# A state-space convolution and attention kernel: filter generation and the first FFT convolution put into one pipeline over chunks of 128 channels

## The chip, the cores and the metric

The kernel runs on one core of a Trainium2 chip. The metric is the device time of that core in microseconds (us), as the median of the runs; all runs quoted here are of the same, undisturbed state, and most runs of one kernel lie within 0.5%. The engines are named as the profile names them: PE (TensorE, matrix multiplication; PEld is its weight load), DVE (VectorE), ACT (ScalarE), POOL (GpSimd). SP issues DMA.

## The reference, cut to what matters

Sequence length 2048, 512 channels, 128 complex modes per channel, 32 heads of 16, all in bf16. The output is four residual layers in a row: a state-space convolution A, a sliding-window attention B, the same A again, the same B again.

```python
def _A_ref(u, ...):                       # u is layernorm(x)
    dt = exp(log_dt)
    K = einsum("dn,dnl,dn->dl", C, exp(dt*A*l), dt*B).real    # filter: 512 channels x 2048 taps
    y = irfft(rfft(u padded to 2L) * rfft(K padded to 2L))[:L]
    return y + u * Dskip
def _B_ref(x, wqkv, wo):                  # window of 8 positions, step 2
    ...
x = x + A(ln(x)); x = x + B(ln(x)); x = x + A(ln(x)); x = x + B(ln(x))
```

The filter K is the same in both A layers, so it is made once.

## The kernel before

A tap index l is split as l = x + 32·y, so that a power of the mode is a product of two table entries: table X has the powers 0 to 31, table Y the 64 powers in steps of 32 (with the coefficient folded in). For each channel, K is a small matrix product of Y and X with the 128 modes as the contraction. The tables are made on VectorE by doubling: level `lev` makes entries m..2m−1 from entries 0..m−1 by one complex multiplication, which is four products and two sums.

```python
def dbl_level(T, lev, lad0, dsl):              # 128 channels at a time
    m = 1 << lev
    for e0 in range(0, m, HALF):
        for (r_out, m_a, m_b, op) in ((0, Mr, Mi, ALU.subtract), (1, Mi, Mr, ALU.add)):
            nc.vector.tensor_tensor(ta, T[:, :, 0, e0:e0+mm, :], m_a, ALU.mult)
            nc.vector.tensor_tensor(tb_, T[:, :, 1, e0:e0+mm, :], m_b, ALU.mult)
            nc.vector.tensor_tensor(T[:, :, r_out, m+e0:m+e0+mm, :], ta, tb_, op)

for dc in range(4):                            # kgen: all four chunks of 128 channels
    for lev in range(6): dbl_level(Y, lev, 5, dsl)
    for dch in range(128):                     # contraction, 2 weight loads and matmuls per channel
        nc.tensor.matmul(psk[:, dl, :], Y[:, dh, 0, :, d2], X[:, dh, 0, :, d2], start=True,  stop=False)
        nc.tensor.matmul(psk[:, dl, :], Y[:, dh, 1, :, d2], Xin[:, dh, :, d2],  start=False, stop=True)
    ...                                        # X of the next chunk; k_fft of the chunk before
```

Only when all of K's spectrum is there does the first convolution begin. A transform of 128 channels has a first step (`s1`: 32 matmuls, then copies `Z` out of PSUM) and a second step (`s2`: 16 or 32 PE transposes, a copy `zt`, DFT matmuls with constants `C2`, 512 columns each). The kernel before does the second step in quarters (`cg` counts 16 of them), and lets each quarter's product and inverse follow on the next quarter's forward transform:

```python
for cg in range(17):                            # a_layer, both convolutions
    if cg < 16:
        if c == 0: Z = fft_s1_chunk(...)
        xp = fft_s2_sub(nc, P, C, Z, c)         # 8 transposes, zt, 4 DFT matmuls
        cur = (cg,) + pointwise(cg, xp)         # xc on ACT, pa and pb on DVE
    if pend is not None: inverse_s2(*pend)      # the quarter before
    pend = cur
# then one last stage for all channels, 32 matmuls of 512 plus the skip term T = U*Dskip and X
```

## Time and profile before

The median of the kernel before is 824.7 us in the runs beside the changed kernel (823.9 in the first three). In the stage table below, stage ends are read from the copies that write X in the timeline.

| stage of the profiled execution | from | to | length, us |
|---|---|---|---|
| ladder of powers | 0 | 68 | 68 |
| tables and contraction | 68 | 281 | 213 |
| last filter transform and convolution 1 | 281 | 403.3 | 122 |
| attention 1 | 403.3 | 554.6 | 151.3 |
| convolution 2 | 554.6 | 666.2 | 111.6 |
| attention 2 and store | 666.2 | 826.0 | 159.8 |

The busy line of the page of the kernel before gives averages over all these stages:

```profile
PE 526.4 (64%) x4796; PEld 345.1 (42%) x4848; DVE 583.6 (71%) x989; ACT 314.5 (38%) x368; POOL 6.3 (1%) x5
```

The windows view of the kernel before gives the same by stage. Its columns are named in its first line: each engine's busy us, with the number of instructions in brackets, then the granted PE clock as a share of full speed, the share of DMA engines busy, and GB/s.

```profile
core 0: us, PE busy (x) PEld busy (x) DVE busy (x) ACT busy (x) POOL busy (x), PEclk, DMA share, GB/s
68.00:281.00 213.00, 112.52 (x1357) 93.03 (x1360) 174.14 (x266) 65.22 (x67) 0.00 (x0) 1.00 0.00 1
281.00:403.00 122.00, 94.36 (x745) 66.05 (x753) 85.41 (x187) 57.51 (x81) 6.06 (x1) 0.97 0.17 65
554.60:666.20 111.60, 80.86 (x631) 56.56 (x640) 64.23 (x112) 42.75 (x58) 0.00 (x0) 0.86 0.13 53
```

In the first stage DVE is busy 174 of 213 us: it bounds table building. In the two convolutions no engine is full (PE, the busiest, 77% and 72%). The timeline of the kernel before, PE only, shows two more things (columns: start, duration, engine, line, operation; in brackets the idle time before it and what ended it): a contraction pair, one matmul of the real and one of the imaginary part, and the first matmul of convolution 2.

```profile
105.25 0.21 PE L381 MATMUL psk<-Xtab,Ytab 128*64 128x32 bf16 x1
105.30 0.21 PE L382 MATMUL psk<-Xin,Ytab 128*64 128x32 bf16 x1
...
570.71 1.01 PE L162 MATMUL ps_s_5152<-U_5042,F1sb 128*128 128x128 bf16 x8 [17.40 <-DMA F1sb<-c_F]
```

One weight load with its matmul starts every 53 ns. Convolution 2 starts 16 us after attention 1's last copy, and waits for a DMA of a constant that stands behind the 4 MB filter.

### The profile page before, as it was taken

To read this page: it belongs to the slowest core of one execution; us is meant where nothing else is said; L and a number is where in the kernel's file an instruction comes from. 1 tells how busy PE (TensorE), PEld (TensorE's weight loads), DVE (VectorE), ACT (ScalarE), POOL (GpSimd) and SP (SyncE) were. 2 spreads that over 40 slices of the span, in tenths; PEclk is the share of its full clock that TensorE was granted. 3 is DMA by queue.
4 is the path that set the end of the run, shared out by engine and by line. 5 is a ranking of instruction groups with operands and counts; after the bars stand their busy time and mean duration, and the time that the engine had idled before them with its cause. 6 is when DMAs were issued, how large, how long until landed. Compare 5 with 4: busy or idle time off the path is not lost.

```text
span 826.0 us, 11334 instructions
## 1 busy us (share of the span) xinstructions
PE 526.4 (64%) x4796; PEld 345.1 (42%) x4848; DVE 583.6 (71%) x989; ACT 314.5 (38%) x368; POOL 6.3 (1%) x5
## 2 busy tenths in 40 slices
PE   0200176565655757888699718962888859971996
PEld 0100174462643735665345513432666534551343
DVE  0899979979797367666925989685666373598961
ACT  0431025244152345444564322351444446432234
POOL 0000000000000000002000000000000000000000
PEclk9999999999999999999899859995999969985999
DMA  9000000000000024002000300015000000030011
GB/s 208 8 0 0 0 2 1 1 1 1 2 0 1 2 102 204 1 1 77 27 1 2 90 1 0 1 58 247 2 1 2 1 0 1 2 90 1 0 52 52
DMA packets 8655, 25.61 MB, mean 31 GB/s; under 512 B 4446, under 2 KB 5982, under 8 KB 7518
## 3 DMA queue, kind: packets, MB, share of 16 engines
q1 hardware_dynamic: 4828, 18.16, 6.5%
q10 hardware_dynamic: 3776, 6.72, 2.8%
q8 instruction: 38, 0.62, 0.3%
q14 instruction: 13, 0.11, 0.0%
HBM read 14.95 MB, written 6.29 MB: 26 GB/s over the span
## 4 chain that ended last, share of the span: by engine, by line
PE 44%; DVE 33%; ACT 10%; issue 6%; DMA 6%; ACTq 0%; DVEq 0%; SPq 0%
PE ps_qk L512 7%; DVE ta L313 6%; DVE tb L314 6%; DVE Ytab L315 5%; PE po L623 5%; PE psk L381 3%; PE psk L382 3%; PE ps_v L525 3%; DMA F1sb<-c_F 3%; PE ps_o L640 3%; DVE prodpv L617 2%; ACT xc L220 2%; PE Lp L555 2%; ACT KTq L383 2%; PE vp L234 2%
## 5 line engine op out<-in xcount | busy, mean ns | idle before, releaser
L381 PE MATMUL psk<-Xtab,Ytab 128*64 128x32 bf16 x512 | 56.5, 213 | 83.9 <-issue 60.6
L623 PE MATMUL po<-prodpv,sb_ident 128*128 128x512 bf16 x248 | 66.5, 399 | 35.5 <-DVE prodpv L609 31.3
L381 PEld LDWEIGHTS <-Ytab 128*64 128x64 bf16 x512 | 55.4, 157 | 73.8 <-issue 61.0
L382 PEld LDWEIGHTS <-Ytab 128*64 128x64 bf16 x512 | 55.0, 156 | 27.8 <-DVE Ytab L315 14.0
L382 PE MATMUL psk<-Xin,Ytab 128*64 128x32 bf16 x512 | 56.4, 214 | 13.6 <-DVE Ytab L315 13.6
L512 PE MATMUL ps_qk<-xnT,wqk 128*128 128x512 bf16 x248 | 58.2, 386 | 4.8 <-ACT xnT L499 3.9
L383 ACT CAST KTq<-psk 64x1024 bf16<-64x1024 f32 x16 | 16.1, 1006 | 104.1 <-PE psk L382 104.1
L623 PEld LDWEIGHTS <-sb_ident 128*128 128x128 bf16 x256 | 25.8, 101 | 67.4 <-issue 45.4
L609 DVE TENSOR_TENSOR prodpv<-V,Lsb 128x2048 bf16<-128x2048 bf16 (+1 forms) x40 | 42.2, 1113 | 16.3 <-PE po L623 16.1
L220 ACT CAST xc<-xp 128x1024 bf16<-128x1024 f32 x32 | 32.4, 1012 | 33.6 <-PE xp L188 33.6
L315 DVE TENSOR_TENSOR Ytab<-ta,tb 128x2048 bf16<-128x2048 bf16 (+4 forms) x56 | 42.9, 765 | 1.9
L555 PE MATMUL Lp<-sb_bones,prodqk 128*128 128x8 bf16 x1024 | 34.5, 167 | 12.6 <-DVE prodqk L551 7.2
L178 PE MATMUL pt<-sb_ident,Z 128*128 128x128 bf16 x384 | 39.5, 256 | 4.5 <-ACT Z L361 2.7
L555 PEld LDWEIGHTS <-prodqk 128*128 128x128 bf16 x1024 | 32.3, 98 | 21.7 <-DVE prodqk L551 8.7
L178 PEld LDWEIGHTS <-Z 128*128 128x128 bf16 x384 | 32.4, 117 | 17.9 <-issue 8.0
L512 PEld LDWEIGHTS <-wqk 128*128 128x128 bf16 x256 | 25.3, 100 | 33.9 <-issue 6.9
L234 PE MATMUL vp<-sb_IC,pb 128*128 128x256 bf16 x128 | 36.5, 285 | 3.0 <-DVE pb L224 3.0
L233 PE MATMUL vp<-sb_IC,pa 128*128 128x256 bf16 x128 | 36.4, 284 | 1.8 <-DVE pa L223 1.8
L358 PEld LDWEIGHTS <-F1Ksb 64*128 64x128 bf16 x256 | 27.1, 139 | 24.7 <-issue 20.7
L640 PE MATMUL ps_o<-wo_t,oT 128*128 128x512 bf16 x124 | 32.3, 379 | 6.9 <-ACT o L626 4.3
L235 PE MATMUL vp<-sb_IC,pb 128*128 128x256 bf16 x128 | 36.1, 282 | 0.0
L236 PE MATMUL vp<-sb_IC,pa 128*128 128x256 bf16 x128 | 35.9, 281 | 0.0
(350 smaller groups left out, 1220.2 us busy)
## 6 DMA issues: line engine op xcount, KB each, us to landing
kt_scratch<-Kt_81 SPq DMA_DIRECT2D x1, 4096.0 KB, 12.1
Kt<-kt_scratch SPq DMA_DIRECT2D x1, 4096.0 KB, 14.8
Vp<-V SPq DMA_DIRECT2D x2, 1568.0 KB, 9.0
F1Tsb<-c_F1T ACTq DMA_DIRECT2D x2, 1024.0 KB, 11.4
F1sb<-c_F SPq DMA_DIRECT2D x2, 1024.0 KB, 12.2
F1Ksb<-c_F1K ACTq DMA_DIRECT2D x1, 1024.0 KB, 16.9
wqk<-in_B_wqkv_dram SPq DMA_DIRECT2D x1, 1024.0 KB, 5.7
X_70<-in_A_u_dram SPq DMA_DIRECT2D x1, 512.0 KB, 7.6
```

The source lines that it names most:

```text
L178: nc.tensor.transpose(pt[:, r, g, :], Z[:, r, c * 4 + g, :], ident[:])
L220: nc.scalar.copy(xc[:], xp[:])
L234: nc.tensor.matmul(o, P2, IC[:, 1, :], start=False, stop=False)
L313: nc.vector.tensor_tensor(ta[:, :, 0:mm, :], T[:, :, 0, e0:e0 + mm, :], m_a, ALU.mult)
L314: nc.vector.tensor_tensor(tb_[:, :, 0:mm, :], T[:, :, 1, e0:e0 + mm, :], m_b, ALU.mult)
L315: nc.vector.tensor_tensor(T[:, :, r_out, m + e0:m + e0 + mm, :], ta[:, :, 0:mm, :], tb_[:, :, 0:mm, :], op)
L381: nc.tensor.matmul(psk[:, dl, :], Y[:, dh, 0, :, d2], X[:, dh, 0, :, d2], start=True, stop=False)
L382: nc.tensor.matmul(psk[:, dl, :], Y[:, dh, 1, :, d2], Xin[:, dh, :, d2], start=False, stop=True)
L512: nc.tensor.matmul(ps[:, sc * 512:(sc + 1) * 512], wqk[:, ct, which * 512 + ft * 128: which * 512 + (ft + 1) * 128], xnT[:, ct, s0:s0 + 51 ...
L555: nc.tensor.matmul(Lp[f2][:, w, jj, :], pr[:, f2, jj * 128:(jj + 1) * 128], bones[:], start=True, stop=True)
L623: nc.tensor.matmul(po[jj // 2][:, jj % 2, :], ident[:], p2[:, jj, :], start=(w == 0), stop=(w == W - 1))
L640: nc.tensor.matmul(ps[:, jj, :], oT[:, ft, j * 128:(j + 1) * 128], wo_t[:, ft, :], start=(ft == 0), stop=False)
```

## The change

The intent: hide the first convolution under table building, which leaves PE idle for about half of the time and ACT for more, and make the tables cheaper.

1. Chunks of 128 channels go through one pipeline: tables of the two halves (64 channels each), transform of U, transform of K of the chunk before, and the last part (product, inverse, last matmuls) of the chunk before.
2. The split is now l = y + 64·x. Table Y's last two levels (16 entries to 64) are not doubled but left as unsummed products: the 16 base entries times three multipliers, once by the real part and once by the imaginary part. The sum of the two happens in the contraction, as two more matmuls into the same PSUM cells.
3. The contraction uses 32-column weights in four column groups.
4. The skip term goes into K's spectrum (one matmul with a row of ones), so T and its matmuls go away.
5. K passes through DRAM once to change its layout; the spectrum goes to DRAM for convolution 2, and is loaded after the constants there.

The diff, cut to its core:

```diff
-            for lev in range(6):
-                dbl_level(Y, lev, 5, dsl)
+        for lev in range(4):
+            self.double(Y, 1 << lev, lev, hc)
+        for q, lev in ((1, 4), (2, 5), (3, LV48)):          # y_products
+            nc.vector.tensor_tensor(Y[.. q*EYB:(q+1)*EYB ..], src, self.mult(self.MA, lev, hc, EYB), ALU.mult)
+            nc.vector.tensor_tensor(Y2[.. (q-1)*EYB:q*EYB ..], src, self.mult(self.MB, lev, hc, EYB), ALU.mult)
 ...
+        for ds in range(16):                                # contract, 64 channels
+            for m in range(4):
+                for g in range(4):
+                    d = g * 16 + ds
+                    xs = X[:, m // 2, h, :, t]
+                    if m % 2 == 0:
+                        nc.tensor.matmul(psk[32*g:32*g+32, ds, :], xs, Y[:, m // 2, h, :, t], ...)
+                    else:
+                        nc.tensor.matmul(psk[32*g:32*g+32, ds, EYB:], xs, Y2[:, 1 - m // 2, h, :, t], ...)
 ...
+        for dc in range(4):
+            def mid(dc=dc):
+                xcs[dc] = cv.u_fft(dc, rstd, nb, "act")
+                return k_fft(dc - 1) if dc > 0 else None
+            Kt = half(dc * 2, mid)      # tables of 64 channels, then mid, then the contraction
+            if dc > 0:
+                cv.finish(dc - 1, xcs.pop(dc - 1), Kt)
+            half(dc * 2 + 1)
+        Kt = k_fft(3)
+        cv.finish(3, xcs.pop(3), Kt)
 ...
+    def s2(self, Z, dst, what):                             # second step of every transform
+        for ch in range(2):
+            pt = self.pst([128, 2, 2, 4, 128], BF)
+            ...                                             # 16 transposes into pt
+            self.evac("zt", zt, pt)                         # ACT (DVE in convolution 2)
+            for c2 in range(2):
+                xp = self.pst([128, 2, 512])
+                ...                                         # 4 DFT matmuls of 512 columns
+                self.evac(what, dst[:, ch * 2 + c2, :, :], xp[:])
 ...
-        a_layer(nc, tc, C, Xg, Kt0)      # convolution 1, after all of kgen
+        for dc in range(4):              # convolution 2, now chunk by chunk
+            xc = cv.u_fft(dc, rstd, nb, "dve")
+            cv.finish(dc, xc, Kts[dc])
```

What stands ahead of what on PE is decided when the kernel is built, and in these traces it follows the order of the program text: when e4 below moves one transform in the text, the even halves shrink by about 10 us and the odd ones grow by 14.

## The prediction

> **What bounds the kernel now** (span 826.0 us). The windows view splits it: prologue and ladder 0–68, tables and contraction 68–281, last filter transform and first convolution 281–403, attention to about 554, second convolution to 666, attention to 826. In 68–281 VectorE is busy 174 of 213 us while PE and ACT wait: one 128-channel chunk costs about 54 us. Convolution 1 runs after all chunks (285–403), with no engine full: in 316–386 PE 59, DVE 48, ACT 32 of 70 us. Convolution 2 waits 17.4 us (timeline) for its F1 table, queued behind the 4 MB filter load.
>
> **What changes.** (a) Y levels 16 and 32 become six unsummed products: per 128 channels 12 operations of 128x2048 (1.22 us each in the groups view) instead of 18, and X's first level becomes a copy. I sum 21 us of DVE per 64 channels, 42 per 128. (b) Convolution 1 moves under table building: it adds pa/pb (8 x 0.69 us per chunk) to DVE; all evacuations and the normalization go to ACT, my sum about 36 us per chunk. (c) Contraction: 256 weight-load/matmul pairs per 64 channels instead of 128. Now a pair takes 53 ns in the timeline with 64 columns; the Trainium skill ("TensorE: Matmul & The Clock Gate", LDWEIGHTS) gives columns/1.2 ns, which agrees: 53.3. 32 columns in four column groups, which "TensorEngine Tiling (Array Packing)", Key Properties, says run in parallel, should give 28–45 ns, so 7–12 us per half. (d) K passes through DRAM, about 5 us, exposed only for the last chunk. (e) Dskip enters the spectrum: no T tensor (4 x 1.2 us DVE, 16 matmuls of 512 per layer). (f) log_dt is loaded first, not landing at 23.
>
> **Critical path.** Not simply DVE. Y has one buffer, so Y(h+1) waits for contraction h; and PE's order puts one U transform and one K transform before every even contraction. Those are evacuation-bound on ACT (25–27 us with the normalization) and, as the K transforms in the profile run with cold matmuls (N=512 every 0.43 us), perhaps 32 us. So I expect DVE to stall about 15 us per chunk, a period near 62–65 us per chunk instead of 54, not the DVE-bound 48. The scheme still removes convolution 1 as a stage (about 118 us). Ladder end near 60 us; last contraction near 300; tail (K DMA, K transform 3, finish 3) 33 us: fused stage ends near 330 (now 403): −73.
> Attention 1: layer norm needs all four channel chunks of X, so it no longer overlaps the last stage (it did at 391–403): +6.
> Convolution 2: F1 is loaded before the filters, first matmul about 9 us earlier; chunkwise final stage, fewer matmuls: 112 -> about 95: −17.
> Attention 2: unchanged (it already waited until 665).
> Sum: 823.9 − 73 + 6 − 17 = about 740 us.
>
> **Prediction: 740 us, 80% range 705–775; faster by over 2% 0.95, within 2% 0.04, slower 0.01.**
>
> **What would show it.** Fused stage ending 305–350; DVE in it with idle time before the Ytab copy released by PE psk; psk pairs 28–45 ns apart; pa/pb inside the table stage; ACT about 36 us per chunk; convolution 2's first matmul 8 us after attention 1 instead of 16.
>
> **What would make it wrong.** Column groups not overlapping (contraction 13 us: +20); transforms warm and scheduling smooth (DVE-bound: fused stage 290, −40); strided PSUM writes or the 16-element ACT evacuations costing more than counted; the ladder slowed by three more table loads.

## The result and the profile after

The changed kernel is correct and takes 748.9 us (747.1 to 749.6, 4 runs) against 824.7 us. The ratio is 0.908, with a 95% interval of 0.906 to 0.910. Ratios here and below are the mean time of one kernel's fast runs over that of the kernel before in the same rounds, so not quite the ratio of the medians that are quoted.

| stage | before | after | difference | predicted |
|---|---|---|---|---|
| to the end of convolution 1 | 403.3 | 309.7 | −93.6 | −73 |
| attention 1 | 151.3 | 163.3 | +12.0 | +6 |
| convolution 2 | 111.6 | 113.4 | +1.8 | −17 |
| attention 2 | 159.8 | 160.5 | +0.7 | 0 |
| span of the profiled execution | 826.0 | 746.9 | −79.1 | −84 |

The total came out 9 us from the prediction. Three of its four terms did not: the fused stage gained 20 us more, and convolution 2 and attention 1 together gave back 25 us more. The errors cancel. So there are three things to explain.

The busy line of the page and the windows view of the changed kernel:

```profile
PE 479.3 (64%) x5863; PEld 304.3 (41%) x5908; DVE 506.0 (68%) x936; ACT 363.3 (49%) x436; POOL 8.4 (1%) x21
```

```profile
55.40:272.90 217.50, 129.82 (x2869) 92.79 (x2879) 171.34 (x304) 123.75 (x156) 2.09 (x16) 0.79 0.10 33
272.90:309.70 36.80, 23.63 (x180) 17.31 (x181) 6.22 (x10) 18.86 (x21) 0.96 (x1) 0.72 0.12 44
473.00:586.40 113.40, 79.26 (x716) 59.89 (x720) 66.64 (x168) 50.45 (x61) 0.00 (x0) 0.85 0.13 55
```

The first line is tables and contraction with most of convolution 1 beneath: about as long as table building alone was before, with DVE no fuller than before (171 of 217.5 us). The second is the tail after the last contraction. The granted clock is 0.79 and 0.72 there, and e9 below shows that it matters. The 1.00 and 0.97 of the kernel before must not be set against it. In its first stretch, under a column that reads 1.00, the DFT matmuls of its K transforms start 0.43 us apart:

```profile
138.60 0.63 PE L186 MATMUL xp<-zt,sb_C_64 128*128 128x512 bf16 x1
139.03 0.63 PE L187 MATMUL xp<-zt,sb_C_64 128*128 128x512 bf16 x1
```

That is the slow pace, called cold here; the fast one, called warm, is 0.215 us. The clock record of that trace begins only at 307 us, and the column reads 1.00 where there is no record. Over that kernel's other runs the mean clock lies between 0.84 and 0.93, at times within 1% of each other. So the distance between starts of equal matmuls is the safer sign. Counted from the timelines, the kernel before has 21 cold starts and no warm one in that first stretch, and 11 cold and 38 warm in the stretch of convolution 1; the changed kernel has 40 cold and 25 warm between its second and its last contraction.

The waits view of the changed kernel, DVE, up to the end of the fused stage (engine, line waiting, what it waited for: us in total, times, longest):

```profile
DVE pa L250 <- ACT Kt L173: 38.5, 8, 22.7
DVE Ytab L433 <- PE psk L461: 21.5, 3, 7.2
```

`Ytab` has one buffer and waits for the contraction, as predicted. The wait of `pa` for the transform of K was not named in the prediction; 22.7 us of it is one wait in the tail, where no tables are left to build. The contraction's end is marked by its copy `KTq` on ACT. The timeline of the changed kernel, ACT, four consecutive copies:

```profile
102.02 1.01 ACT L464 CAST KTq<-psk 128x1024 bf16<-128x1024 f32 x1 [5.11 <-PE psk L461]
...
141.11 1.01 ACT L464 CAST KTq<-psk 128x1024 bf16<-128x1024 f32 x1 [4.16 <-PE psk L461]
...
160.28 1.01 ACT L464 CAST KTq<-psk 128x1024 bf16<-128x1024 f32 x1 [3.17 <-issue]
...
197.32 1.01 ACT L464 CAST KTq<-psk 128x1024 bf16<-128x1024 f32 x1 [3.75 <-PE psk L461]
```

An even half, which has the two transforms ahead of its contraction on PE, takes 37 to 39 us; an odd half takes 19. A chunk is 56 to 58 us, where 62 to 65 was predicted. The windows view of the first of these chunks, its even half and then its odd half:

```profile
102.00:141.10 39.10, 25.45 (x403) 17.21 (x405) 23.96 (x43) 28.12 (x35) 0.23 (x2) 0.67 0.05 15
141.10:160.30 19.20, 14.52 (x379) 11.91 (x379) 18.79 (x35) 10.19 (x15) 0.38 (x2) 1.00 0.25 84
```

DVE is idle for 15 us of the even half and for almost nothing of the odd one. The contraction itself, PE in the timeline of the changed kernel:

```profile
136.26 0.24 PE L458 MATMUL psk<-Ytab,Xtab 128*32 128x64 bf16 x4
136.30 0.24 PE L461 MATMUL psk<-Y2tab,Xtab 128*32 128x48 bf16 x4
136.35 0.24 PE L458 MATMUL psk<-Ytab,Xtab 128*32 128x64 bf16 x4
```

Eight pairs of weight load and matmul start in 0.09 us, so one in 11 to 12 ns. All 256 take 4.5 to 4.7 us in the first half of a chunk, of which about 2 us is a single gap that the profile puts down to issue (in the second half 5.6 us, with two such gaps). Predicted were 28 to 45 ns per pair and 7 to 12 us.

### The profile page after: what moved, and what is told of

Same layout as the page of the kernel before. It is cut to its first block, busy times and chain, and to the rows that moved or that the text cites. A ratio compares the mean times of both kernels' runs of the same rounds, so it can differ in the third digit from the quotient of the medians.

```text
span 746.9 us, 13529 instructions
## 1 busy us (share of the span) xinstructions
PE 479.3 (64%) x5863; PEld 304.3 (41%) x5908; DVE 506.0 (68%) x936; ACT 363.3 (49%) x436; POOL 8.4 (1%) x21
## 4 chain that ended last, share of the span: by engine, by line
PE 45%; DVE 29%; ACT 15%; issue 8%; DMA 3%; ACTq 0%; DVEq 0%
PE ps_qk L599 8%; PE po L710 5%; PE ps_o L727 4%; ACT Z L173 4%; PE ps_v L612 4%; ACT zt L173 4%; PE ps L198 3%; DVE ln_stats L134 3%; PE ps L203 2%; DVE Ytab L442 2%; DVE prodpv L704 2%; PE ps L205 2%; PE ps L206 2%; PE Lp L642 2%; DVE Y2tab L444 2%
## 5 line engine op out<-in xcount | busy, mean ns | idle before, releaser
L134 DVE BATCH_NORM_STATS2 ln_stats<-X 128x6 f32<-128x512 bf16 x64 | 43.0, 709 | 30.5 <-PE ps_o L727 12.3
L173 ACT CAST Z<-ps 128x1024 bf16<-128x1024 f32 x48 | 45.8, 1025 | 25.0 <-PE ps L185 25.0
L198 PE MATMUL ps<-sb_ident,Z 128*128 128x128 bf16 x384 | 35.4, 265 | 33.4 <-ACT Z L173 33.4
L203 PE MATMUL ps<-zt,sb_C_99 128*128 128x512 bf16 x48 | 25.2, 525 | 43.0 <-ACT zt L173 32.4
L173 ACT CAST xc<-ps 128x1024 bf16<-128x1024 f32 x32 | 31.9, 1013 | 41.7 <-PE ps L206 41.7
L642 PE MATMUL Lp<-sb_bones,prodqk 128*128 128x8 bf16 x1024 | 34.5, 167 | 12.7 <-DVE prodqk L638 7.2
L173 ACT CAST VT<-ps 128x512 bf16<-128x512 f32 x48 | 26.5, 587 | 30.5 <-PE ps L238 30.5
L642 PEld LDWEIGHTS <-prodqk 128*128 128x128 bf16 x1024 | 32.2, 98 | 21.8 <-DVE prodqk L638 8.7
L458 PE MATMUL psk<-Ytab,Xtab 128*32 128x64 bf16 x1024 | 22.6, 208 | 26.7 <-DVE Ytab L442 18.0
L236 PE MATMUL ps<-sb_IC,pb 128*128 128x256 bf16 x128 | 35.2, 275 | 1.0 <-DVE pb L251 1.0
L235 PE MATMUL ps<-sb_IC,pa 128*128 128x256 bf16 x128 | 35.3, 276 | 0.7 <-DVE pa L250 0.7
L237 PE MATMUL ps<-sb_IC,pb 128*128 128x256 bf16 x128 | 35.1, 274 | 0.0
L238 PE MATMUL ps<-sb_IC,pa 128*128 128x256 bf16 x128 | 35.0, 274 | 0.0
L173 ACT COPY zt<-ps 128x2048 bf16<-128x2048 bf16 x16 | 29.8, 1865 | 7.6 <-PE ps L198 7.4
```

Of the source, the lines that this page charges most:

```text
L134: nc.vector.bn_stats(stats[:, jj, :], Xt[:, jj, :])
L173: self.nc.scalar.copy(dst, src)
L198: nc.tensor.transpose(pt[:, c2, r, g, :], Z[:, r, (ch * 2 + c2) * 4 + g, :], ident[:])
L203: nc.tensor.matmul(xp[:, 0, :], C2[:, 0, :], zt[:, c2, 0, :], start=True, stop=False)
L235: nc.tensor.matmul(o, pa[:, 0, sl], IC[:, 0, :], start=True, stop=False)
L236: nc.tensor.matmul(o, pb[:, 1, sl], IC[:, 1, :], start=False, stop=False)
```

## The experiments

Eleven kernels were run, all correct. Each is the changed kernel with the edit shown or named. The table has all of them; stages are in us, read from the profiled execution as above. Builds with the very same fused stage end it at 309.7, 310.5, 311.8 and 313.9, so a stage's end is good to some 4 us there, and the other stages to about 1.

| kernel | median | ratio to before | end of conv. 1 | attention 1 | conv. 2 |
|---|---|---|---|---|---|
| before | 824.7 | 1 | 403.3 | 151.3 | 111.6 |
| after | 748.9 | 0.908 | 309.7 | 163.3 | 113.4 |
| e1 group order | 750.9 | 0.910 | 313.1 | 163.4 | 114.1 |
| e2 conv. 2 by whole chunks | 752.9 | 0.912 | 310.5 | 163.4 | 115.9 |
| e3 attention start | 745.9 | 0.904 | 313.9 | 156.9 | 114.0 |
| e4 U transform moved | 761.2 | 0.922 | 321.4 | 162.7 | 114.6 |
| e5 no overlap | 839.6 | 1.019 | 400.2 | 162.9 | 114.5 |
| e6 doubling | 759.9 | 0.922 | 321.1 | 163.3 | 114.4 |
| e7 second step two deep | 696.7 | 0.845 | 274.4 | 164.6 | 96.9 |
| e8 conv. 2 finely interleaved | 742.7 | 0.901 | 311.8 | 163.2 | 105.5 |
| e9 idle matmuls added | 729.5 | 0.883 | 292.3 | 164.9 | 110.4 |
| e10 = e7 + e3 | 690.9 | 0.838 | 275.1 | 156.9 | 96.4 |
| e11 = e10 + e8 + tail | 692.8 | 0.840 | 278.4 | 158.3 | 95.1 |

### e5: how much is overlap, how much is cheaper tables

```diff
-        for dc in range(4):
-            ...  # mid, half, finish, half as above
+        for hc in range(8):
+            half(hc)
+        for dc in range(4):
+            xc = cv.u_fft(dc, rstd, nb, "act")
+            Kt = k_fft(dc)
+            cv.finish(dc, xc, Kt)
```

> The changed kernel with the overlap undone: all eight halves of tables and contractions first, then for each chunk transform of U, transform of K, last part. Same work. It parts the gain into cheaper tables and overlap. Theory A (VectorE needs about 42 us of tables per chunk, 44 with the contraction between; the overlap hides the transforms, which as one PE-ACT chain take about 45 us per chunk): tables end near 55 + 4 x 50 = 255 us, the first convolution near 255 + 4 x 42 = 420, the whole near 860 us, slower than the kernel before; so all of the gain and more is overlap. Theory B (the gain is the cheaper tables, the overlap hides little): below 800 us.

It takes 839.6 us, slower than the kernel before. The tables alone now take 20.1 us per half, 40 us per chunk against 54 before (DVE busy 78 of 80 us in four halves, so fully bound by it), but the four chunks of transforms and last parts then take 178.5 us, 44.6 each. Without overlap, the cheaper tables are eaten by transforms and a convolution that run chunk by chunk: the stage ends at 400.2 us, 3 us ahead of the kernel before, and attention 1 then gives back 12. So 90 of the 94 us that the fused stage won come from the overlap. Theory A, with its total put 20 us too high.

### e6: the unsummed products undone

```diff
-        for q, lev in ((1, 4), (2, 5), (3, LV48)):
-            ...                          # 6 products of 128x2048
+        self.double(Y, 16, 4, hc)
+        self.double(Y, 32, 5, hc)
 ...
-            for m in range(4):
+            for m in (0, 2):
```

> The changed kernel with the unsummed products undone: the last two Y levels are built by doubling (18 operations of 0.69 us instead of 6 of 1.22 us per half: 5.1 us more VectorE per half), and the contraction has 128 pairs per half instead of 256. Theory A (the even half is bound by the chain of two transforms through PE and ACT, so VectorE has 14 us of slack there; the odd half is bound by VectorE): 0 to 3 us more per even half, 3 to 5 us per odd half, less about 2 us for each shorter contraction: the fused stage ends 4 to 20 us later. Theory B (VectorE bounds both halves): about 8 x 5 = 40 us later.

The fused stage ends 11.4 us later. Of this 10.1 us comes in the first two halves, where no transform of K competes and DVE bounds (the second `KTq` is at 112.15 instead of 102.02, both read from ACT's timeline). After that, even halves take 34.5 to 35.6 us, some 2.7 us less than the 37.0 to 39.1 of the changed kernel, and odd halves 22.0 to 22.4 instead of 18.9 to 19.2, some 3.2 us more. So the slower tables cost nothing in an even half: what counts there is the contraction, which took 1.8 us instead of 4.6. This is Theory A, and it says that a shorter contraction shortens an even half one for one.

### e4: one transform moved to the other half

```diff
             def mid(dc=dc):
-                xcs[dc] = cv.u_fft(dc, rstd, nb, "act")
                 return k_fft(dc - 1) if dc > 0 else None
             Kt = half(dc * 2, mid)
             if dc > 0:
                 cv.finish(dc - 1, xcs.pop(dc - 1), Kt)
+            xcs[dc] = cv.u_fft(dc, rstd, nb, "act")
             half(dc * 2 + 1)
```

> The changed kernel with one edit in the fused stage: the transform of U of a chunk is issued after the first convolution's last part of the chunk before (so beside the odd half's tables) instead of ahead of the even half's contraction. Same work, same buffers. Theory A (the even half is bound by PE's order: two transforms of about 32 us stand ahead of the even contraction, while VectorE waits for Y): the odd half grows, the even half shrinks from 37 us to about 25, the chunk period goes from 56.3 to 48-53 us and the fused stage ends 10 to 30 us earlier. Theory B (ACT's and PE's sum of work per chunk bounds the stage, whatever the order): the period stays within 2 us of 56.3.

Theory A fell, and Theory B's period within 2 us of 56.3 did not come true either. The even half did shrink, to 27.5 to 28.3 us, but the odd half grew to 32.6 to 34.2, and a chunk takes 61.3 us instead of 57.0 (means of the chunks between the second and the last `KTq`). The end is 11.7 us later. The sum of the transforms is paid in either place. A likely part of the extra is the passage of K through DRAM, some 5 us with nothing beside it on PE now; that part was not tested alone.

### e1: does taking turns make the contraction fast?

```diff
-            for m in range(4):
-                for g in range(4):
+            for g in range(4):
+                for m in range(4):
```

> The changed kernel with one edit: in the contraction the four matmuls of one column group now follow each other, instead of the four column groups taking turns. Result must stay correct. Theory A (the turns let weight load and matmul of different column groups overlap; that is why 256 pairs take about 4.5 us, 17 to 18 ns each): pairs go to 27 ns or more, a contraction takes 7 us or more; as two contractions per chunk stand in the period, the fused stage (now ending at 309.7 us) ends 12 to 25 us later. Theory B (a 32-column weight load with a 64-column matmul simply costs 17 ns, the groups have no part): contraction stays at 4.5 us and the time at 748.9 us within 1%.

The contraction takes 4.6 to 5.2 us instead of 4.5 to 4.7, and the time differs by 0.3%. So the turns are not what makes it fast: with four column groups, narrow pairs are cheap here in either order. Whether the groups overlap at all is not shown by this, as a contraction without column groups was not tried.

### e7: the second step of the transform two groups deep

After e4 and e6, what was left was the chain itself: in a transform PE and ACT take turns. The waits view of the changed kernel, PE, from 103 to 273 us:

```profile
PE ps L203 <- ACT zt L173: 24.0, 12, 2.2
PE ps L198 <- ACT Z L173: 12.4, 6, 2.8
```

PE waits 2 us for each copy `zt`. The second 16 transposes do not depend on it, but stand behind the DFT matmuls that do.

```diff
         for ch in range(2):
             pt = self.pst([128, 2, 2, 4, 128], BF)
             ...                                       # 16 transposes
             self.evac("zt", zt, pt)
+            zts.append(zt)
+        for ch in range(2):
+            zt = zts[ch]
             for c2 in range(2):
                 ...                                   # 4 DFT matmuls, evacuation
```

> The changed kernel with one edit in the second step of every transform: both groups of 16 transposes are issued before the first DFT matmuls, so that PE transposes the second half while ACT copies the first. No work is added or removed. Theory A (each half of the fused stage and each chunk of convolution 2 is bound by a chain in which PE and ACT take turns; in it PE waits about 2 us for each of two copies): a transform gets 2 to 3 us shorter, the chunk period goes from 56.3 to 50-53 us, the tail and each chunk of convolution 2 lose 2 us each: 15 to 30 us in all. Theory B (ACT's sum of evacuations, or VectorE, bounds): less than 5 us.

696.7 us: 52 us less than the changed kernel, where 15 to 30 were expected of it. Theory A, but undersized. The fused stage ends at 274.4 and convolution 2 takes 96.9 us. The waits and windows views of this kernel (same columns; PE from 103 to 273, then DVE to 290, then the fused stage from the second contraction to the last):

```profile
PE ps L207 <- ACT zt L173: 4.2, 7, 1.3
```

```profile
DVE Ytab L437 <- PE psk L465: 5.8, 3, 2.8
```

```profile
101.80:243.60 141.80, 103.65 (x2310) 78.52 (x2308) 125.78 (x221) 102.30 (x128) 1.45 (x10) 0.88 0.14 47
```

The same stretch of work took 170.9 us in the changed kernel. DVE is now busy 126 of 142 us, at 46 to 49 us per chunk. The windows view of the first chunk, even half and odd half, shows what bounds each: ACT the even half (busy 27.0 of 27.5 us), DVE the odd one (18.5 of 18.9):

```profile
101.80:129.30 27.50, 19.30 (x406) 14.35 (x405) 23.84 (x43) 26.99 (x36) 0.23 (x2) 0.89 0.07 21
129.30:148.20 18.90, 14.56 (x380) 11.90 (x379) 18.49 (x34) 10.19 (x16) 0.38 (x3) 1.00 0.25 86
```

But PE's waits for `zt` fell by 20 us in this stage and the stage by 29. The rest shows in the DFT matmuls. First the changed kernel's timeline of PE in one transform of K, then this kernel's in one transform of U:

```profile
127.90 0.59 PE L203 MATMUL ps<-zt,sb_C_99 128*128 128x512 bf16 x1 [2.01 <-ACT zt L173]
128.71 0.63 PE L205 MATMUL ps<-zt,sb_C_99 128*128 128x512 bf16 x1 [0.22 <-issue]
129.14 0.63 PE L206 MATMUL ps<-zt,sb_C_99 128*128 128x512 bf16 x1
```

```profile
108.86 0.38 PE L207 MATMUL ps<-zt,sb_C 128*128 128x512 bf16 x1 [1.31 <-ACT zt L173]
109.08 0.38 PE L208 MATMUL ps<-zt,sb_C 128*128 128x512 bf16 x1
```

Starts are 0.43 us apart in the first and 0.215 us in the second. The Trainium skill ("TensorE: Matmul & The Clock Gate", section "Wait — 56ns, not 53.3ns?") gives 426.7 ns for 512 columns on a cold array and 215.7 ns on a warm one, and this trace agrees with both. The two transforms shown are of different kinds, but the count agrees: 7 cold and 72 warm starts in this stretch, where the changed kernel had 40 and 25. That PE was cold because it took turns with ACT is what e9 tests.

### e9: the clock by itself

Order and waits cannot be told apart from the clock in e7, so work was added to the changed kernel instead: four matmuls in each wait for `zt`, their result overwritten.

```diff
                 xp = self.pst([128, 2, 512])
+                if c2 == 0:
+                    for _ in range(4):
+                        nc.tensor.matmul(xp[:, 0, :], C2[:, 0, :], self.C["IC"][:, 0:2, :], start=True, stop=True)
```

> The changed kernel with work added: in the wait of PE for each copied group of transposes stand four more matmuls of 512 columns, whose result is overwritten. The order, and with it the waits for ACT, stay. They take 0.9 us warm or 1.7 us cold in a wait of about 2 us. It asks what part of the 52 us that the deeper second step won is the clock. Theory A (mostly the clock: with its gaps filled PE keeps the fast clock, and the DFT matmuls go from 0.43 to 0.216 us each): the granted clock in the fused stage rises from about 0.8 to 0.9 or more, and the whole gets 15 to 40 us faster although work was added. Theory B (mostly the waits that the reordering took away): the time stays within 5 us of 748.9 or grows.

729.5 us: 19 us faster with 96 more matmuls of 512 columns. The windows view of the changed kernel from its second contraction to its last, then that of this kernel over the same stretch of work, and its PE timeline with the added matmuls (L205) ahead of the DFT matmuls:

```profile
102.00:272.90 170.90, 113.11 (x2301) 81.46 (x2308) 126.18 (x221) 104.74 (x128) 1.46 (x10) 0.80 0.11 39
```

```profile
102.10:259.60 157.50, 111.09 (x2349) 79.58 (x2356) 125.37 (x220) 103.26 (x128) 1.47 (x10) 0.90 0.13 42
```

```profile
128.05 1.03 PE L205 MATMUL ps<-sb_IC,sb_C 128*128 128x512 bf16 x4
130.24 0.38 PE L206 MATMUL ps<-zt,sb_C 128*128 128x512 bf16 x1 [1.17 <-ACT zt L173]
130.46 0.38 PE L207 MATMUL ps<-zt,sb_C 128*128 128x512 bf16 x1
```

The stretch shortens from 170.9 to 157.5 us (e7: 141.8), and the granted clock there from 0.80 to 0.90; 2 cold and 72 warm starts are left. Theory A. What exactly lets PE go cold stays open: between two groups of DFT matmuls lie not only the 2 us of waiting but also 16 transposes (1.1 us warm, 1.9 cold), and no run tells whether these keep PE warm. So in the fused stage about half of e7's gain is the clock (17 of 35 us at the end of convolution 1), and in convolution 2 little (3 of 16.5 us).

### e2 and e8: convolution 2

```diff
-        for dc in range(4):                       # e2
-            xc = cv.u_fft(dc, rstd, nb, "dve")
-            cv.finish(dc, xc, Kts[dc])
+        prev = None
+        for dc in range(5):
+            xc = cv.u_fft(dc, rstd, nb, "dve") if dc < 4 else None
+            if prev is not None:
+                cv.finish(dc - 1, prev, Kts[dc - 1])
+            prev = xc
```

> The changed kernel with one edit, in the second convolution alone: the transform of chunk n+1 is issued before the last stage of chunk n, as the kernel before had it in effect. Theory A (convolution 2 did not get its 17 us because its four chunks run one after the other on PE, ACT and DVE with drained pipelines between the parts): convolution 2, now 113.6 us from the end of attention 1 to its last X evacuation, shortens by 8 to 18 us, and the whole by as much. Theory B (it is the number of evacuations, or the cold matmuls, that bounds each part, so order has no part): less than 3 us.

Theory A did not come true in this form: convolution 2 took 115.9 us. A likely reading, not tested by itself, is that a whole transform placed ahead of a whole last part is still two blocks in a row on each engine. So the grain was made finer in e8, with `finish` cut into steps:

```diff
+        for dc in range(4):                       # e8, convolution 2
+            Z = cv.s1(lambda j: U[:, j, :])
+            if last is not None:
+                last()                            # last matmuls of the chunk before
+            step, last = cv.parts(dc, xc, Kts[dc])
+            if dc < 3:
+                U = cv.u_norm(dc + 1, rstd, nb, "dve")
+            cv.s2(Z, xc, "xc", step)              # step(c): product of quarter c, inverse of c-1
+            step(4)
```

> The changed kernel with one edit, in the second convolution alone: as in the kernel before, the product and the inverse of each quarter of a chunk follow directly on the forward transform of the next quarter, the next chunk's normalization is ahead of them, and a chunk's last matmuls stand after the next chunk's first. Same work. Theory A (convolution 2 lost its gain because forward and inverse no longer overlap within a chunk; moving whole chunks, the earlier run, could not show it as engines run in order): convolution 2 goes from 113.5 to 90-100 us, the whole by 13 to 23 us. Theory B (one of its engines, or the cold clock, bounds it): less than 5 us.

Convolution 2 takes 105.5 us, 8 less: in the direction of Theory A and short of its size. The waits view of PE in convolution 2 says why e7 did more. First the kernel before, from 554 to 667 us, then the changed kernel, from 483 to 587:

```profile
PE ps_s_5152 L162 <- DMA F1sb<-c_F: 17.4, 1, 17.4
...
PE xp L185 <- DVE zt L183: 1.4, 4, 0.4
```

```profile
PE ps L185 <- DVE ln_mvb L138: 11.6, 1, 11.6
PE ps L203 <- DVE zt L171: 10.6, 8, 1.4
PE ps L198 <- ACT Z L173: 8.7, 4, 2.5
```

The kernel before waited 1.4 us for `zt` in the whole layer, the changed one 10.6, and 8.7 for `Z`. In e7 the wait for `zt` is 1.3 us and that for `Z` still 8.7; in e8 it is the other way round, 10.8 for `zt` and 1.2 for `Z`. So convolution 2 lost its gain to PE's waits within each chunk, mostly those inside the second step, partly the separation of forward and inverse. That the layer norm of all 16 rows now stands ahead of the first matmul is the first line: it starts 10.4 us after attention 1 (before: 16), where 8 was predicted.

### e3: the start of attention 1

The timeline of the changed kernel after the last copy of convolution 1:

```profile
308.74 6.06 POOL L126 MEMSET Vp<- 1x7168 bf16 x1 [92.04 <-PE ps L264]
...
311.76 0.66 DVE L134 BATCH_NORM_STATS2 ln_stats<-X 128x6 f32<-128x512 bf16 x1
312.34 2.49 DVE L138 CAST ln_mvb<-ln_mv 128x8 bf16<-128x8 f32 x1
312.40 2.43 DVE L134 BATCH_NORM_STATS2 ln_stats<-X 128x6 f32<-128x512 bf16 x1
317.10 2.19 DVE L119 COPY wv<-wvn 128x512 bf16<-128x512 bf16 x4 [2.27 <-DMA wvn<-in_B_wqkv_dram]
...
321.24 1.01 PE L584 MATMUL pt_x<-sb_ident,xn 128*128 128x128 bf16 x8 [12.61 <-DVE xn L152]
```

A cast of 8 columns that takes 0.15 us elsewhere takes 2.49, and both stretched operations end when the POOL memset does (308.74 + 6.06 = 314.8). The same statistics operation takes 0.66 us beside the memset just before, so it is the cast that is held, and the next operation behind it. The Trainium skill ("SBUF — State Buffer", section "Who interferes with whom") says that a VectorE operation in a two-port mode, which a cast can enter, and a GpSimd operation block each other for a whole instruction. That is in keeping with this, though the profile does not show the mode and no run here took the memset away by itself. In the kernel before, the memset (at 385 us) and most of the layer norm's statistics fell beside the last stage of convolution 1. The four copies stood after it there too (at 405.65), but did not wait for their DMA.

```diff
-    nc.gpsimd.memset(Vp[0:1, 2:NJ, :], 0.0)
+    nc.sync.dma_start(Vp[0:1, 2:NJ, :], zero.ap())       # zero: a constant tensor
 ...  # and the four wv<-wvn copies stand after the layer norm of attention 1
```

> The changed kernel with two edits at the start of attention 1: row 0 of Vp is cleared by a DMA from a zero tensor instead of a POOL memset, and the reordering copies of wv stand after the layer norm instead of ahead of it. Theory A (attention 1 grew by 11.5 us because both now stand between the last X evacuation and the layer norm: the memset stretches two DVE operations to 2.4 us each, and the copies wait for their DMA): the first transposes of xn start 6 to 10 us earlier than 11.5 us after the last X evacuation, attention 1 goes from 163.1 to 153-157 us, the whole by 6 to 10 us. Theory B (the growth is only the layer norm that lost its overlap, as predicted): less than 3 us.

Attention 1 takes 156.9 us, 6.4 less, and its first transposes start 5.4 us after convolution 1's last copy instead of 11.5. The median of the whole fell by only 3.0 us, where 6 to 10 were expected; its fused stage ended 4.2 us later in the profile, within the spread of builds named above. On top of e7 the same edit gave 7.7 us in attention 1 and 5.8 us in the median (e10). So about half of attention 1's growth of 12 us goes with the memset and the copies, and the other half, which was predicted, with the layer norm that lost its overlap: the first long run of `ps_qk` matmuls begins 14.2 us after the last copy of convolution 1 in the kernel before, and 20.0 in e3.

### e10 and e11: the best kernel

> The second step two groups deep (696.7 us) and the earlier start of attention 1 (its attention 1 was 6.4 us shorter) together. If the two act on separate stages, as argued, the gains add: 690 us, 687 to 693.

690.9 us, as expected: the gains add. This is 0.838 of the kernel before and 58 us below the changed kernel.

> All of these together: the second step two groups deep, the earlier start of attention 1, the fine interleaving in convolution 2 (alone it won 6 to 8 us), and the same interleaving for the last chunk of the fused stage, whose tail after the last contraction now takes 31 us. If convolution 2's two edits take away the same waits, it gains little over the two edits before: 685 to 690 us; if they add, 676 to 684 us. The tail should lose 4 to 7 us.

692.8 us, outside both ranges and no better than e10: convolution 2 goes only from 96.4 to 95.1 us, and the tail did not shrink (32.2 us from the last `KTq` to the end of convolution 1, and 30.8 in e10). The fine interleaving won 8 us alone and almost nothing on top of e7. They do not take away the same waits: in convolution 2 of e11 that for `zt` is 1.3 us and that for `Z` 1.1 (e10: 1.3 and 8.7). Waits for `pa` (3.9 us) and 2 us more of PE busy time (74.2 instead of 72.3) stand in their place, and the rest is not explained. The expectation of 4 to 7 us for the tail was wrong.

## Why the prediction was right or wrong, point by point

- **What bounds the kernel, and that overlap is the gain: right.** e5 shows that without overlap nothing is left.
- **The kind of bound, "Not simply DVE": right.** The wait of `Ytab` for the contraction is there, DVE is idle for 12 to 15 us of an even half where a stall of 15 was said, and ACT's 36 us per chunk measured 37 to 38. The wait of `pa` for the K transform, 15 us in three chunks, was not foreseen.
- **The fused stage, −73 predicted, −94 measured.** The prediction's period is a sum, DVE's work ("the DVE-bound 48") plus a stall of "about 15 us". The stall came out near its size. The term that was mis-sized is DVE's work: 43 to 44 us in the first two full chunks, the tables 39 (e5) instead of 42. An odd half, where DVE is busy 18.8 of 19.2 us, shows it undisguised: half of 48 would be 24, and its tables alone were put at 21. Three chunks at 57 us instead of 62 to 65 are 15 to 24 us, most of the 20 (an estimate from these numbers); the ladder ended 5 us earlier than the 60 said, and the tail took 37 us instead of 33. The contraction was mis-sized too, 4.6 us in an even half and 5.6 in an odd one instead of "7–12 us per half"; e6 shows that it counts one for one in an even half, but how much of the 20 us it is was not separated. The named rival, a contraction of 13 us because column groups do not overlap, did not come true.
- **Cold transforms, "perhaps 32 us": right in the number, and not followed up.** The two transforms ahead of an even contraction take 32 to 34 us. The prediction used the cold 0.43 us per matmul as a fact of the stage. The K transforms were cold before the change too, as it says, but most of convolution 1 was warm and is so no longer. With the waits filled by matmuls (e9), 19 us come back.
- **Attention 1, +6 predicted, +12 measured.** The lost overlap of the layer norm was right. The step missed: the POOL memset and the loading of weights, which used to fall inside convolution 1, now stand in front of the attention, and with them the copies that wait for the load (e3: 6.4 us for all).
- **Convolution 2, −17 predicted, +2 measured: wrong.** The first matmul came 10.4 us after attention 1 instead of 8. The failing step is "chunkwise final stage, fewer matmuls: 112 -> about 95". PE's busy time fell only from 80.9 to 79.3 us, and PE's new waits for `zt` and `Z` (19 us) took the gain back. With those for `zt` removed (e7) the stage takes 96.9 us, close to what had been predicted.
- **The sum, 740 against 748.9,** is near because the first error and the other two have opposite signs.

What stays open: the gap of about 2 us labelled issue inside most contractions, the spread of 4 us between builds of the same fused stage, how much of attention 1's 6.4 us is the memset and how much the copies, and what holds convolution 2 at 95 us in e11.

## What to carry to other kernels

Overlap pays where one engine is full and others are idle, but a chain in which PE and ACT take turns can replace the old bound: issue the next independent group of PE work before the work that waits for a copy, at the grain of one copy and not of a whole chunk. Read the granted clock by stage, and check it against the distance between starts of equal matmuls, since here the column read 1.00 over a stage of cold ones. With waits of 2 us, none of them large, part of every transform ran at half pace here, and filling them was worth 19 us even with useless work. When a stage is moved under another, list what used to be hidden beside it, for that now stands in the open.

## What the Trainium skill lacked or had wrong

- "TensorE: Matmul & The Clock Gate" says in "Wait — 56ns, not 53.3ns?" that start to start never drops below about 25 ns. With 32-column weights in four column groups a weight load and matmul started every 11 to 12 ns in this trace. The same page's Part 3, "Measured speedup vs the span model", gives about 4 ns per tile for matmuls packed into different tiles, so the floor is not for those; what is lacking is a pace for a long stream of weight loads and matmuls in column groups.
- "TensorE: Matmul & The Clock Gate", in "Why this matters for your kernels", warns of PE-idle gaps over about 3 us. Here no gap between the second and the last contraction is as long (those in a transform are 1.3 to 2.8 us), and part of the matmuls of every transform still ran cold (0.43 us a start). If transposes do not count as work, the stretches come to 3 us and more, and the warning fits; no run here tells. No page has a case of useless matmuls put into a wait; here they raised the granted clock from 0.80 to 0.90 and saved 19 us.
- No page times a POOL memset of one partition. Its 7168 bf16 elements took 6.06 us here; a cast of 8 columns beside it took 2.49 us instead of 0.15, and a statistics operation 0.66, as elsewhere.
